# Sliding-window attention and token MLP, two layers: block-diagonal head pairs, 64-key blocks, transposed outputs, and one scheduled dependency graph

## The chip, the core and the metric

The kernel runs on one core of a Trainium2 chip. The metric is the device time of one execution in microseconds (us). A core has five engines that run on their own and meet through semaphores: TensorE (PE in the profile, its weight loads PEld), VectorE (DVE), ScalarE (ACT), GpSimd (POOL) and SyncE (SP), which issues most of the DMA here. The profile also gives the clock that TensorE was granted, as a share of full speed.

## The reference, cut to what matters

All data is bfloat16. Tokens S = 2048, model width D = 512.

```python
def _A_ref(x, wqkv, wo):                    # attention
    H = 32; Dh = D // H; W = 256            # 32 heads of 16; a query sees itself and the 255 tokens before it
    q, k, v = split_heads(x @ wqkv)
    scores = einsum("bhqd,bhkd->bhqk", q, k) * Dh ** -0.5
    p = softmax(where(mask, scores, -1e9))
    return merge_heads(einsum("bhqk,bhkd->bhqd", p, v)) @ wo

def _B_ref(x, w1, b1, w2, b2):              # MLP over the token axis
    h = layernorm(x)
    u = gelu(einsum("bsd,sf->bdf", h, w1) + b1)      # S -> F = 1792
    return transpose(einsum("bdf,fs->bds", u, w2) + b2)

x = A_x
x = x + _A_ref(layernorm(x), ...); x = x + _B_ref(layernorm(x), ...)
x = x + _A_ref(layernorm(x), ...); x = x + _B_ref(layernorm(x), ...)
```

The attention works token by token within a window, so its stages can be interleaved over chunks of tokens. The first product of the MLP sums over all tokens: it ends only after the last token of the attention is done.

## The kernel before

A layer is recorded stage by stage: normalisation, transposes, value, query and key projections for all tokens; then attention; then the output projection; then the MLP. Every engine gets its instructions in the order in which they are recorded, and waits for the semaphores of what it reads.

The attention works on blocks of 128 keys, two heads at a time. Each block meets three query blocks (384 queries), of which the first and the third are masked by triangles. A head has only 16 dimensions, so query and key weights are padded to 32 rows per head, which doubles the projection, and two heads' scores run in two 32-row groups of the array.

```python
                    for uidx, (g, c, hp) in enumerate(units):     # group of 4 heads, key block, pair
                        nj = min(3, NT - c)
                        def f_sc(e, g=g, c=c, nj=nj, hp=hp, st=st):
                            last = None
                            for hl in range(2):
                                hh = 2 * hp + hl
                                last = e.matmul(
                                    SC[:, 2 * st + hl, 0:nj * P],
                                    lhsT=kT_sb[32 * hh:32 * hh + DH, g, c * P:(c + 1) * P],
                                    rhs=qT_sb[32 * hh:32 * hh + DH, g, c * P:(c + nj) * P],
                                    start=True, stop=True, tile_position=(32 * hh, 0))
                        ...   # exp of both heads' scores, 768 columns, on ScalarE
                        ...   # first query block: triangle multiply on VectorE
                        ...   # third query block: affine_select on GpSimd
                        pvq.append((g, c, hp, nj, rs))
                        if len(pvq) > 4:
                            emit_pv(*pvq.pop(0))                  # values, 17 columns per head: 16 and the sum
```

(Cuts are marked with "...".) In the value product the probabilities are the weights that are loaded, and 17 columns per head stream: the output comes with queries on the partitions, and has to be transposed again before the output projection. The gelu of the MLP is made of two ScalarE and four VectorE instructions.

The softmax here doesn't subtract the row's maximum and nothing guards it: scores larger than these inputs give would overflow.

## Time and profile before

The time before is 834.89 us, median of 3 runs (833.97 to 837.9).

| stage of layer 1 | us | what fills it | granted clock |
|---|---|---|---|
| normalisation, transposes, projections | 0 to 112 | loads, then TensorE | 1.00 |
| attention | 112 to 290 (178) | ScalarE | 0.50 |
| output projection | 290 to 314 (24) | VectorE (21.1 us busy) | 0.91 |
| normalisation | 314 to 325 (11) | VectorE | 0.70 |
| MLP | 325 to 432 (107) | TensorE | 0.98 |

The page of the kernel before, part 2. The span is cut into 40 slices, and each digit is the busy share of an engine in tenths; the row PEclk is the granted clock in tenths.

```profile
PE   0499989999999985989968998999999999499898
...
DVE  6740036666666695444557000666666667834322
ACT  0026699999999842330010667999999994233100
...
PEclk9999975555555598999987999555555557899999
```

TensorE looks busy from end to end. But the clock row has two stretches of 5, and in just those ScalarE is at 9: these are the two attentions. The same is told by busy time per stretch. Columns are busy us with the number of instructions for PE, PEld, DVE, ACT and POOL, then granted clock, DMA share, GB/s.

```profile
core 0: us, PE busy (x) PEld busy (x) DVE busy (x) ACT busy (x) POOL busy (x), PEclk, DMA share, GB/s
20.00:110.00 90.00, 76.89 (x368) 36.35 (x368) 27.69 (x63) 38.98 (x67) 0.00 (x0) 1.00 0.00 1
112.00:290.00 178.00, 174.53 (x1958) 85.01 (x1959) 114.15 (x512) 172.97 (x258) 90.98 (x224) 0.50 0.05 13
290.00:314.00 24.00, 20.79 (x120) 10.00 (x117) 21.14 (x43) 10.31 (x18) 0.00 (x0) 0.91 0.00 1
325.00:432.00 107.00, 97.94 (x443) 43.43 (x441) 48.02 (x104) 21.55 (x33) 0.00 (x0) 0.98 0.44 118
```

In attention ScalarE is busy 173 of 178 us. In all other stages it has time, and in attention TensorE works at half clock on little. The timeline of the attention (start, duration, instructions merged, with the count last) shows the pace.

```profile
179.56 7.14 ACT L409 ACTIVATE pT<-SC 128x768 bf16<-128x768 f32 x10
179.72 0.50 PE L399 MATMUL SC<-qT,kT 16*128 16x384 bf16 x2
...
180.15 0.33 PE L366 MATMUL OA<-v,pT 128*128 128x17 bf16 x6
...
180.42 0.50 PE L399 MATMUL SC<-qT,kT 16*128 16x384 bf16 x2
```

Two 384-column scores overlap in 0.50 us, and the six value matmuls follow 0.43 us after the scores start. Ten exponentials take 7.14 us; less the 0.81 us of the last one, nine periods are 6.33 us, so the period of a unit is 0.70 us, one exponential of 768 columns. The groups of instructions give the cost of one: busy us in all, mean ns of one, then idle time before.

```profile
L409 ACT ACTIVATE pT<-SC 128x768 bf16<-128x768 f32 x448 | 316.8, 808 | 4.4 <-PE SC L399 4.4
...
L334 PE MATMUL prj<-xhT,wq_sb 128*128 128x512 bf16 x256 | 65.7, 379 | 0.0
```

### The profile page before, as it was taken

How to read it: one execution, taken by the hardware profiler on the slowest of the kernel's cores; microseconds unless marked ns; L12 is line 12 of the kernel's file. 1: busy time of each engine (PE TensorE's matmuls, PEld its weight loads, DVE VectorE, ACT ScalarE, POOL GpSimd, SP SyncE). 2: the span in 40 equal slices, each digit the busy share in tenths (PEclk: the TensorE clock that was granted, in tenths of full speed). 3: DMA queues.
4: the chain of work that ended last, by engine and by line, in shares of the span. 5: the costliest groups of instructions: out<-in, count | busy, mean ns of one | idle time of the engine just before them, and what ended most of it. 6: DMA issues, size and time to landing. Idle time of an engine off the chain costs nothing. (4 is left out here: it accounts for less than half of the span.)

```text
span 836.1 us, 16132 instructions
## 1 busy us (share of the span) xinstructions
PE 749.4 (90%) x5824; PEld 354.5 (42%) x5824; DVE 432.2 (52%) x1482; ACT 491.1 (59%) x752; POOL 193.7 (23%) x463
## 2 busy tenths in 40 slices
PE   0499989999999985989968998999999999499898
PEld 0244434444444442434434443444444444244343
DVE  6740036666666695444557000666666667834322
ACT  0026699999999842330010667999999994233100
POOL 5000035555555300000000000555555550000000
PEclk9999975555555598999987999555555557899999
DMA  9000030000000001563500002100000000036446
GB/s 201 0 1 1 1 101 2 2 2 2 2 3 2 2 0 28 154 159 89 157 19 1 1 1 60 42 3 2 2 2 2 2 2 1 1 101 168 109 138 189
DMA packets 67773, 36.69 MB, mean 44 GB/s; under 512 B 4720, under 2 KB 67184, under 8 KB 67696
## 3 DMA queue, kind: packets, MB, share of 16 engines
q1 hardware_dynamic: 63824, 35.65, 15.6%
q0 software_dynamic: 3872, 0.02, 1.1%
q8 instruction: 48, 0.79, 0.4%
q14 instruction: 29, 0.24, 0.1%
HBM read 33.56 MB, written 2.10 MB: 43 GB/s over the span
## 5 line engine op out<-in xcount | busy, mean ns | idle before, releaser
L409 ACT ACTIVATE pT<-SC 128x768 bf16<-128x768 f32 (+2 forms) x512 | 344.7, 768 | 6.1 <-PE SC L399 4.4
L420 POOL TENSOR_SCALAR_AFFINE_SELECT pT<-pT 128x256 bf16<-128x256 bf16 x448 | 182.0, 406 | 497.7 <-DVE pT L415 497.7
L415 DVE TENSOR_TENSOR pT<-pT,mall 128x256 bf16<-128x256 bf16 x512 | 149.2, 294 | 229.6 <-ACT pT L409 217.5
L399 PE MATMUL SC<-qT,kT 16*128 16x384 bf16 (+2 forms) x1024 | 244.1, 474 | 9.5 <-ACT pT L409 5.1
L366 PEld LDWEIGHTS OA<-v,pT 128*128 128x128 bf16 x2880 | 115.7, 105 | 157.8 <-POOL pT L420 133.9
L366 PE MATMUL OA<-v,pT 128*128 128x17 bf16 x2880 | 163.0, 179 | 1.2 <-PE OA L366 0.2
L498 PE MATMUL uacc<-xh_sb,w1buf 128*128 128x512 bf16 x448 | 101.4, 390 | 18.1 <-DVE xh_sb L274 17.8
L539 PE MATMUL yacc<-uT,w2buf 128*128 128x512 bf16 x448 | 99.2, 384 | 8.8 <-DVE uT L518 6.5
L342 ACT ACTIVATE qT<-prj 128x512 bf16<-128x512 f32 x64 | 38.2, 597 | 65.2 <-PE prj L334 65.2
L498 PEld LDWEIGHTS uacc<-xh_sb,w1buf 128*128 128x128 bf16 x448 | 44.6, 100 | 74.9 <-issue 24.3
L539 PEld LDWEIGHTS yacc<-uT,w2buf 128*128 128x128 bf16 x448 | 43.9, 99 | 64.1 <-issue 9.7
L399 PEld LDWEIGHTS SC<-qT,kT 16*128 16x128 bf16 x1024 | 52.7, 99 | 32.2 <-ACT pT L409 6.8
L334 PE MATMUL prj<-xhT,wq_sb 128*128 128x512 bf16 x256 | 65.7, 379 | 0.0
L334 PE MATMUL prj<-xhT,wk_sb 128*128 128x512 bf16 x256 | 65.7, 379 | 0.0
L383 DVE TENSOR_TENSOR o<-OA,rtmp 128x64 bf16<-128x64 f32 x256 | 57.5, 225 | 8.9
L544 DVE SCALAR_TENSOR_TENSOR x_sb<-yacc,b2col,x_sb 128x512 bf16<-128x512 f32 x32 | 24.0, 751 | 65.2 <-PE yacc L539 65.2
L305 PE MATMUL trp<-ident,xh_sb 128*128 128x128 bf16 x128 | 16.5, 310 | 39.5 <-DVE xh_sb L274 27.8
L342 ACT ACTIVATE kT<-prj 128x512 bf16<-128x512 f32 x64 | 38.2, 597 | 17.0 <-PE prj L334 17.0
L256 DVE BATCH_NORM_STATS2 stats<-x_sb 128x6 f32<-128x512 bf16 x64 | 44.0, 688 | 6.5 <-DMA x_sb<-in_A_x_dram 4.9
L503 ACT ACTIVATE t0b<-uacc,b1col 128x512 bf16<-128x512 f32 x28 | 19.2, 687 | 45.7 <-PE uacc L498 45.7
L379 DVE RECIPROCAL rtmp<-OA 128x4 f32<-128x4 f32 x256 | 45.0, 176 | 0.8 <-PE OA L366 0.3
L453 PE MATMUL yp<-wo_sb,oTt 128*128 128x512 bf16 x128 | 37.0, 416 | 6.4 <-DVE x_sb L457 5.8
(42 smaller groups left out, 348.3 us busy)
## 6 DMA issues: line engine op xcount, KB each, us to landing
w1buf<-in_B_w_dram SPq DMA_DIRECT2D x14, 1024.0 KB, 6.1
w2buf<-in_B_w_dram SPq DMA_DIRECT2D x16, 896.0 KB, 5.4
x_sb<-in_A_x_dram SPq DMA_DIRECT2D x4, 512.0 KB, 5.5
out_dram<-x_sb SPq DMA_DIRECT2D x16, 128.0 KB, 2.4
wstage<-in_A_wqkv_dram SPq DMA_DIRECT2D x1, 1024.0 KB, 9.1
wv_sb<-in_A_wqkv_dram SPq DMA_DIRECT2D x1, 512.0 KB, 10.0
wo_sb<-in_A_wo_dram SPq DMA_DIRECT2D x1, 512.0 KB, 10.4
b1col<-in_B_b_dram POOLq DMA_DIRECT2D x1, 7.0 KB, 6.5
```

Of the source, the lines that this page charges most:

```text
L256: S_.op("vector", lambda e, t=t: e.bn_stats(stats[:, t, :], x_sb[:, t, :]), reads=[R(f"x_t{t}")], writes=[R(f"stats{t}")])
L334: last = e.matmul(prj[:, ps, :], lhsT=w_sb[:, c, tq * P:(tq + 1) * P], rhs=xhT_sb[:, c, tb * 512:(tb + 1) * 512], start=(c == 0), stop=(c ...
L342: S_.op("scalar", lambda e, tq=tq, tb=tb, dstT=dstT, ps=ps: e.activation(dstT[:, tq, tb * 512:(tb + 1) * 512], prj[:, ps, :], ACTF.Copy), ...
L366: last = e.matmul(OA[:, slot, hh * (DH + 1):(hh + 1) * (DH + 1)], lhsT=pv[:, hl, j, :], rhs=v_sb[:, c, hidx * (DH + 1):(hidx + 1) * (DH + 1)],
L379: S_.op("vector", lambda e, slot=slot: e.reciprocal(rtmp[:, 0:4], OA[:, slot, 0:4 * (DH + 1)].rearrange("p (h e) -> p h e", e=DH + 1)[:, : ...
L383: S_.op("vector", lambda e, slot=slot, g=g, qb=qb: e.tensor_tensor(o_sb[:, qb, g * 64:(g + 1) * 64].rearrange("p (h e) -> p h e", h=4), OA ...
L399: last = e.matmul(SC[:, 2 * st + hl, 0:nj * P], lhsT=kT_sb[32 * hh:32 * hh + DH, g, c * P:(c + 1) * P], rhs=qT_sb[32 * hh:32 * hh + DH, g, ...
L409: S_.op("scalar", lambda e, nj=nj, rs=rs, st=st: e.activation(pT[:, rs, 0:2 * nj * P].rearrange("p (h n) -> p h n", h=2), SC[:, 2 * st:2 * ...
L415: return e.tensor_tensor(v, v, mall[:, :, 0, :], op=ALU.mult)
L420: return e.affine_select(v, v, pattern=[[0, 2], [-1, P]], compare_op=ALU.is_ge, fill=0.0, base=-1, channel_multiplier=1)
L498: last = e.matmul(uacc[:, us, :], lhsT=w1buf[:, b, sc, tt * P:(tt + 1) * P], rhs=xh_sb[:, sc, :], start=(sc == 0), stop=(sc == NT - 1))
L539: last = e.matmul(yacc[:, ys, :], lhsT=w2buf[:, b, fc, stt * P:(stt + 1) * P], rhs=uT_sb[:, fc, :], start=(fc == 0), stop=(fc == NFT - 1))
```

## The change

The intent is to do less work and to have every engine work in every stage.

1. Heads come in pairs. Keys are kept block-diagonally, 64 keys of one head beside 64 keys of the other, so that 32 rows hold two heads with no padding, and a score matmul gives 2 x 64 keys for N queries. Query and key projections halve.
2. Key blocks have 64 keys, so that fewer masked columns are computed: the exponential streams 307 thousand columns per partition in both layers, not 369 thousand.
3. The values and a block of ones are the loaded weights and the probabilities stream: outputs are transposed already, and the denominators come out spread over the rows. Division is Ln, then Exp(-x), then a multiply. Four 32-column groups of the array work on four head pairs.
4. Attention goes in chunks of 512 tokens. Projections of later chunks, output projections of earlier ones and the MLP outputs of the layer before are recorded as "filler" for TensorE.
5. Smaller changes: gelu is one ScalarE instruction, GpSimd's masks go to VectorE, the results of the query and key projections are copied out by VectorE and no longer by ScalarE, and the inverse root of the normalisation is a power on GpSimd.
6. All operations go into one graph with estimated costs, and a list scheduler sets the order of each engine before the program is built. At each step it takes the operation that can start first, and scores go before values, values before fillers.

The diff, cut to its core:

```diff
-class Sched:
+class Graph:
+    def schedule(self):
+        ...
                if m < INF and (best is None or m < best[0]):
                    pick = None
                    for o, t in zip(cand[e], ests):
                        if t <= m:
                            pr = (o.prio if o.prio is not None else ready[o.idx], o.idx)
                            if pick is None or pr < pick[0]:
                                pick = (pr, o)
+        ...
-                                    lhsT=kT_sb[32 * hh:32 * hh + DH, g, c * P:(c + 1) * P],
-                                    rhs=qT_sb[32 * hh:32 * hh + DH, g, c * P:(c + nj) * P],
+                                for j, q0, n, c0 in runs:
+                                    tkk, jj = tk(j)
+                                    for i, r in enumerate(rr):
+                                        last = e.matmul(
+                                            PS[:, 2 * ts.slot + i, c0 * 64:(c0 + n) * 64],
+                                            lhsT=kbd[32 * r:32 * r + 32, tkk.slot, o, jj, :, :].rearrange("p h n -> p (h n)"),
+                                            rhs=qT[32 * r:32 * r + 32, tq.slot, o, q0 * 64:(q0 + n) * 64],
+                                            start=True, stop=True, tile_position=(32 * r, 0), skip_group_check=True)
+        ...
-                                        OA[:, slot, hh * (DH + 1):(hh + 1) * (DH + 1)],
-                                        lhsT=pv[:, hl, j, :],
-                                        rhs=v_sb[:, c, hidx * (DH + 1):(hidx + 1) * (DH + 1)],
+                                for dst, den in ((tO, False), (tDen, True)):
+                                    for r in range(4):
+                                        tp, ln = lane[(k, r)]
+                                        w = onesbd[:] if den else vbd[:, tkk.slot, jj, 4 * o + r, :]
+                                        last = e.matmul(
+                                            PS[32 * r:32 * r + 32, 4 + dst.slot, q0 * 64:(q0 + n) * 64], lhsT=w,
+                                            rhs=pt[:, tp.slot, ln, c0 * 64:(c0 + n) * 64],
+                                            start=st, stop=True, tile_position=(0, 32 * r), skip_group_check=True)
+        ...
+            prepare(0)
+            prepare(1)
+            for m in range(NC):
+                tos[m] = attention(m, tqs[m], tks)
+                wo_block(m, tos[m]) if m == NC - 1 else None
+                if m + 2 < NC:
+                    prepare(m + 2)
+                if m < NC - 1:
+                    wo_block(m, tos[m])
-        layer_A(0)
-        layer_B(0)
-        layer_A(1)
-        layer_B(1)
```

The value projection is part of it: it puts the two heads of a pair on the two halves of the partitions, with 64-column tiles.

```python
                for hf in range(2):
                    def f_v(e, hf=hf):
                        last = None
                        for c in range(4):
                            for sc in range(2):
                                tok = (2 * sp + sc) * 64
                                last = e.matmul(
                                    PS[64 * hf:64 * hf + 64, 4 + ft.slot, sc * 256:(sc + 1) * 256],
                                    lhsT=xhT[:, tx.slot, c, tok:tok + 64],
                                    rhs=wqkv[:, c, 1024:1536].rearrange("p (r h e) -> p r h e", h=2, e=16)[:, :, hf, :],
                                    start=(c == 0 and sc == 0), stop=(c == 3), tile_position=(0, 64 * hf),
                                    skip_group_check=True)
                        return last
                    op("tensor", f_v, ...)      # cut
```

## The prediction

> **What bounds it now.** The stages run one after another. By busy time per stretch and the timeline, each layer pays about 85 us of normalisation, transposes and projections (first scores at 110 us), 178 us of attention, 24 us of output projection, 10 us of normalisation gap and 107 us of token MLP. In attention ScalarE is full (10.0 of every 10 us): exponentials of 768 columns (808 ns busy) start every 703 ns. TensorE shows as busy too, but at a granted clock of 0.50 and with little in it: two row-packed 384-column scores overlap in 0.50 us. In projections and MLP TensorE is the bound, at clock 1.00, 216 ns per 512-column matmul (four in 0.86 us).
>
> **What the change removes.** Query/key projections without padding: 512 matmuls become 256 (-55 us of TensorE at full clock), and 128 evictions of 597 ns leave ScalarE for VectorE. 64-key blocks: the exponential streams 307 thousand columns, not 369 thousand; 288 calls of 1024, at 703 + 256 x 0.833 = 916 ns (estimate), and some smaller, 137 us a layer, with 32 Ln/Exp calls about 155 us. GpSimd masks and 128 output transposes go. Gelu becomes one ScalarE call.
>
> **What it adds.** Value projection with 64-wide tiles: 512 x 256 columns, twice the stream (+27 us). GpSimd block-diagonal copies, 128 of about 630 ns (from affine selects, 292 ns at 128 and 406 at 256 elements). TensorE in attention at full clock, per layer: scores, two row groups abreast, 32 us; values plus a ones matmul, four column groups abreast, 32 us if packing is perfect. The Trainium skill (TensorE: Matmul & The Clock Gate, Measured speedup vs the span model) gives 3.07x for four row tiles and 2.38x for three column tiles, and no run here shows column packing, so I take 90 us for both with small-matmul overheads. Fillers: 72 us. So some 160 us, and 48 more for MLP output in layer 2. VectorE gets about 150 us a layer. All three engines are loaded nearly alike; I expect the greedy static order to lose 10 to 20%.
>
> **Sum.** Start 17; attention with everything inside 185; last output projection and normalisation, partly hidden, 8; MLP first half 51; layer 2's MLP outputs, preparation and attention merged, 235; 8; 51; 53; end 4: 612 us. The gain is overlap.
>
> **Clock.** The skill's clock-gate part says a busy array is ungated; the trace agrees for dense stretches (1.00) and shows 0.50 in sparse attention. With fillers and full-column values I expect 0.85 or more in the new attention. At 0.50, attention would take 320 us and the gain would vanish.
>
> Predicted 612 us, 8 in 10 within 555 to 690. Faster by over 2%: 0.95; within 2%: 0.02; slower: 0.03.
>
> **What would show it.** First scores before 22 us. Exponentials of 1024 start-to-start near 0.92 us when fed; ScalarE about 370 us busy in total, VectorE 320, GpSimd 110. ScalarE 80 to 90% busy in the first attention, lower in the second, which is TensorE-bound. Mean granted clock over 0.9. Attention of layer 1 takes 170 to 205 us, of layer 2 210 to 260. TensorE dominates the end of the chain of waits, with short DMA waits on MLP weights.
>
> **What would make it wrong.** The clock at half in attention; column-packed matmuls that don't run abreast (over 60 us more per layer); drains at each switch between tilings; VectorE late in freeing PSUM, so that fillers stall; GpSimd copies slower than 630 ns and slowing VectorE.

## More of the kernel before

Sessions differ a little: the kernel before gave medians of 834.6 to 837.9 us from one session to the next, so differences of under 3 us between runs of different sessions are not read.

## The result, and the profile after

The changed kernel takes 610.0 us (median of 4, 605.25 to 611.55), the kernel before 836.39 us in the same rounds. The ratio is 0.727 with a 95% interval of 0.723 to 0.731. Ratios here are the mean time of one kernel's fast runs over that of the other's in the same rounds, so they are not quite the ratio of the medians. The prediction was 612 us.

The page of the changed kernel, part 2:

```profile
PE   4879999999998989989899999999998799998797
...
DVE  5984565765784220036766555874568423001122
ACT  0677798798989411110795996099767951111000
...
PEclk9987999999995799999999999999999579999899
```

The two stretches of 5 in the clock row are gone but for a slice or two each, and only the MLPs, with ScalarE at 1, can still be told apart by eye. By stretches (columns as before; the last of the first attention's exponentials of scores ends at 202.2 us, those of the second run from 292.4 to 493.7 us):

```profile
17.80:203.00 185.20, 170.56 (x2572) 86.21 (x2592) 119.15 (x246) 157.89 (x182) 69.13 (x109) 0.92 0.09 23
203.00:265.50 62.50, 59.89 (x289) 25.49 (x292) 7.30 (x17) 11.68 (x17) 3.02 (x8) 0.98 0.38 101
292.00:475.00 183.00, 173.23 (x2424) 81.87 (x2456) 120.69 (x237) 140.58 (x164) 57.57 (x98) 1.00 0.10 27
475.00:493.00 18.00, 14.55 (x200) 6.23 (x204) 6.17 (x12) 15.90 (x19) 1.05 (x2) 0.51 0.01 2
```

The first attention takes 185 us, hardly more than the 178 us of before, but holds nearly all of its layer's projections and most of the output projection. In the second (292 to 475 us) TensorE is busy 173 of 183 us and ScalarE 141: TensorE has become the bound, with MLP outputs of layer 1 as more filler. The last 18 us of each attention are different: clock 0.51, and VectorE is busy only 6.2 of 18 us (shown for the second). The chain of waits that ended last says the same in shares of the span:

```profile
PE 66%; ACT 15%; DVE 11%; DMA 2%; POOL 2%; issue 2%; DVEq 0%; POOLq 0%
```

Before, that chain could only be followed back through the last MLP; now it reaches through the kernel, and is TensorE for two thirds. The groups of instructions (busy us, mean ns, idle before) show the new exponential and two GpSimd groups:

```profile
L599 ACT ACTIVATE pt<-PS 128x1024 bf16<-128x1024 f32 x288 | 278.5, 1039 | 100.9 <-PE PS L586 88.1 <-PE PS L647 11.9
...
L510 POOL TENSOR_SCALAR kbd<-stg,par 128x512 bf16<-128x512 bf16 x64 | 49.5, 783 | 76.7 <-DVE stg L507 74.7 <-DVE agg L440 1.6
...
L449 POOL TENSOR_TENSOR rstd<-rstd,mhalf 128x1 f32<-128x1 f32 x64 | 37.3, 586 | 4.1
```

The timeline of TensorE in the second attention shows how the small matmuls run. Each row is a group of matmuls with its start:

```profile
353.93 0.32 PE L647 MATMUL PS<-pt,vbd 128*32 128x320 bf16 x4
354.07 0.31 PE L647 MATMUL PS<-pt,onesbd 128*32 128x320 bf16 x4
354.21 0.26 PE L647 MATMUL PS<-pt,vbd 128*32 128x192 bf16 x4
354.29 0.26 PE L647 MATMUL PS<-pt,onesbd 128*32 128x192 bf16 x4
354.48 0.39 PE L586 MATMUL PS<-qT,kbd 32*128 32x128 bf16 x6
354.80 0.29 PE L647 MATMUL PS<-pt,vbd 128*32 128x256 bf16 x4
```

Four value matmuls of 320 columns start at 353.93 us, and the next four 0.14 us later. A 512-column matmul takes 0.216 us at this clock, so one of 320 columns takes 0.135 us: the four column groups run fully abreast. The Trainium skill (TensorE: Matmul & The Clock Gate, Measured speedup vs the span model) has 2.38x for three column tiles; in this stream it is four for one. But from the start of the last group (354.29 us; 192 columns, 0.08 us) to the scores it takes 0.19 us, 0.11 more than its stream. That is the time of a change of tiling; between full-array matmuls that follow each other, the same difference is 3 ns (median). My own count over the trace, from 292 to 475 us, takes each run of matmuls in one tiling, and subtracts from its length the time of its columns:

```
from          to            changes   median extra ns
32-row        full array       78        111
full array    32-row           79        111
32-row        32-column        53        110
32-column     32-row           50        126
```

The program changes tiling 653 times; at 0.11 us that is an estimated 72 us of TensorE's time in the kernel's 610. The Trainium skill says of it (TensorEngine Tiling (Array Packing), Key Properties): "Changing tiling mode (not just tile) drains the TensorE". The trace agrees and adds the size.

### The profile page after: what moved, and what is told of

Read it like the earlier page. It is cut to its first block, busy times and chain, and to the rows that moved or that the text cites. A ratio compares the mean times of both kernels' runs of the same rounds, so it can differ in the third digit from the quotient of the medians.

```text
span 609.5 us, 13842 instructions
## 1 busy us (share of the span) xinstructions
PE 556.2 (91%) x6171; PEld 262.6 (43%) x6240; DVE 300.4 (49%) x610; ACT 341.9 (56%) x400; POOL 150.0 (25%) x266
## 4 chain that ended last, share of the span: by engine, by line
PE 66%; ACT 15%; DVE 11%; DMA 2%; POOL 2%; issue 2%; DVEq 0%; POOLq 0%
PE PS L721 15%; PE PS L707 14%; ACT pt L599 13%; PE PS L586 10%; PE PS L523 8%; PE PS L647 8%; PE PS L499 7%; DVE stats L438 4%; PE PS L673 2%; DVE x_sb L676 2%; DVE pt L620 1%; POOL rstd L449 1%; DVE pt L618 1%; DMA w1b<-in_B_w_dram 1%; DVE xh_sb L451 1%
## 5 line engine op out<-in xcount | busy, mean ns | idle before, releaser
L599 ACT ACTIVATE pt<-PS 128x1024 bf16<-128x1024 f32 (+1 forms) x304 | 290.7, 1028 | 102.9 <-PE PS L586 90.1
L586 PE MATMUL PS<-qT,kbd 32*128 32x320 bf16 (+4 forms) x1440 | 123.3, 267 | 13.6 <-ACT pt L599 10.5
L721 PE MATMUL PS<-uT,w2b 128*128 128x512 bf16 x428 | 106.4, 384 | 10.7 <-DMA w2b<-in_B_w_dram 5.0
L707 PE MATMUL PS<-xh_sb,w1b 128*128 128x512 bf16 x436 | 101.2, 384 | 3.0 <-DVE xh_sb L451 1.0
L620 DVE TENSOR_TENSOR pt<-pt,ldm 128x1024 bf16<-128x1024 bf16 (+2 forms) x104 | 64.4, 619 | 56.7 <-ACT pt L599 56.5
L647 PE MATMUL PS<-pt,vbd 128*32 128x320 bf16 (+4 forms) x1440 | 87.6, 273 | 4.9 <-DVE pt L618 1.8
L647 PE MATMUL PS<-pt,onesbd 128*32 128x320 bf16 (+4 forms) x1440 | 84.0, 270 | 0.0
L499 PE MATMUL PS<-xhT,wqkv 128*128 128x512 bf16 x229 | 68.3, 391 | 5.6 <-issue 4.0
L510 POOL TENSOR_SCALAR kbd<-stg,par 128x512 bf16<-128x512 bf16 x64 | 49.5, 783 | 76.7 <-DVE stg L507 74.7
L523 PE MATMUL PS<-wqkv,xhT 128*64 128x256 bf16 x512 | 56.8, 281 | 1.5 <-DVE xhT L490 1.0
```

Of the source, the lines that this page charges most:

```text
L499: mm_group(ft, 4, lambda e, c: e.matmul(PS[:, 4 + ft.slot, :], lhsT=wqkv[:, c, which * 512 + o * P:which * 512 + (o + 1) * P], rhs=xhT[:, ...
L510: op("gpsimd", lambda e, h=h: e.tensor_scalar(kbd[:, tk.slot, o, :, h, :], stg[:, ts.slot, :].rearrange("p (s n) -> p s n", n=64), par[:, ...
L523: last = e.matmul(PS[64 * hf:64 * hf + 64, 4 + ft.slot, sc * 256:(sc + 1) * 256], lhsT=xhT[:, tx.slot, c, tok:tok + 64], rhs=wqkv[:, c, 10 ...
L586: last = e.matmul(PS[:, 2 * ts.slot + i, c0 * 64:(c0 + n) * 64], lhsT=kbd[32 * r:32 * r + 32, tkk.slot, o, jj, :, :].rearrange("p h n -> p ...
L599: return e.activation(pt[:, tp.slot, la:lb + 1:lb - la, 0:n], PS[:, 2 * ts.slot:2 * ts.slot + 2, 0:n], ACTF.Exp, scale=SMSCALE)
L620: return e.tensor_tensor(v, v, msk.unsqueeze(1).unsqueeze(1).to_broadcast([P, lanes, n, w]), op=ALU.mult)
```

## The experiments

All gave the reference's result within its tolerance. Times are medians of 4 runs; the ratio is to the kernel before in the same rounds, and the changed kernel has 0.727.

| run | us | ratio | what it does |
|---|---|---|---|
| serial | 758.5 | 0.906 | no interleaving of stages on TensorE |
| act_more | 633.9 | 0.756 | 61 us more of ScalarE |
| pe_more | 655.7 | 0.783 | 64 us more of TensorE |
| dve_more | 610.3 | 0.728 | 69 us more of VectorE |
| valt | 590.5 | 0.708 | value projection's halves alternate |
| last_dup | 620.3 | 0.744 | last chunk's scores twice |
| last_full | 616.3 | 0.736 | last chunk: useless full-array matmuls |
| switch / noswitch | 622.6 / 612.1 | 0.746 / 0.734 | 192 more changes of tiling / none more |
| valt_ylate | 586.1 | 0.700 | valt, last MLP outputs start later |
| spread | 565.9 | 0.676 | valt_ylate, fillers spread into the last chunk |
| unpacked | 621.6 | 0.742 | values: column groups not neighbours |

### Is the gain overlap, or cheaper work?

The theory is that the fillers run in the gaps of the attention; the rival, that the attention and the projections merely became cheaper. A phase number keeps TensorE from starting a filler inside an attention chunk, and the other way round. Nothing else changes.

```diff
                     t = max(ready[o.idx], free[e])
+                    if e == "tensor" and o.phase != now:
+                        t = INF
...
+                g.phase += 1
                 tos[m] = attention(m, tqs[m], tks)
+                g.phase += 1
```

> Edit: TensorE may not mix stages: it finishes all projections and fillers recorded before an attention chunk, then that chunk alone, then the fillers after it. The instructions, their number and their costs stay. Theory (the gain is overlap: fillers run in the gaps of an attention that ScalarE paces, and they keep the clock up): about 755 us, 720 to 800, granted clock near 0.5 inside the attention chunks. Rival (the attention and the projections simply got cheaper, and the interleaving matters little): under 680 us.

It took 758.5 us. Of the 226 us that the change gained, 148 come from interleaving, and 78 are left when the new arithmetic runs stage by stage. Busy time per stretch of this run: preparation alone, one attention chunk's middle, and the MLP.

```profile
90.00:100.00 10.00, 9.95 (x67) 5.65 (x69) 7.13 (x12) 0.00 (x0) 8.81 (x14) 1.00 0.01 2
230.00:270.00 40.00, 34.07 (x488) 14.88 (x484) 11.85 (x20) 34.12 (x39) 0.00 (x0) 0.50 0.01 2
280.00:330.00 50.00, 48.45 (x218) 20.95 (x220) 1.53 (x6) 9.40 (x14) 1.55 (x4) 1.00 0.47 126
```

In the chunk ScalarE is busy 34 of 40 us, at clock 0.50 and with TensorE "busy" 34 of 40 us as well. In the preparation ScalarE has nothing to do, and in the MLP 9 of 50 us. So a stage-by-stage order pays for both engines in turn. What the half clock alone costs here no run shows; as ScalarE is busy 85% of the chunk, at most the other 15% could be won from it.

### Which engine bounds it?

The prediction said that VectorE, ScalarE and TensorE are loaded nearly alike. Three runs add work to one engine each.

```diff
+# act_more: beside each exponential
+op("scalar", lambda e, td=td: e.activation(scr[:, td.slot, 0:128], ident[:], ACTF.Copy), ..., after=[prev_sc[0]])
+# dve_more: beside each exponential, a multiply of 256 columns to scratch on "vector"
+# pe_more, in f_sc:
-for j, q0, n, c0 in runs:
+for j, q0, n, c0 in runs * 2:
```

> Edit: beside each of the 304 exponentials one more ScalarE copy of 128 columns to scratch, 60 to 85 us of ScalarE in all. If ScalarE bounds both attentions: all of it comes back, +60 to +85 us. My theory (ScalarE and TensorE both near full in the first attention, TensorE alone in the second): +20 to +45 us.

> Edit: every score matmul is issued twice, the second overwriting the first with the same values: 57 us more of streaming at full clock, two row groups abreast. My theory (TensorE bounds the second attention and shares the first): +40 to +60 us. If ScalarE alone bounds attention: under +15 us. If a denser array keeps the clock up at the ends of both attentions, some 5 us of it come back.

> Edit: beside each exponential one more VectorE multiply of 256 bf16 columns to scratch, about 0.29 us each, 88 us of VectorE in all. The prediction said all three engines are loaded nearly alike: then +40 us or more. The profile shows VectorE 62 to 65% busy in attention: then +5 to +25 us, by late evictions only.

(The 57 us in the expectation of pe_more are too few: all 307 thousand columns, two abreast, are 64 us at full clock.) ScalarE's busy time rose by 61 us and the kernel took 24 us longer, so 39% of it showed. Of the 64 us of TensorE 46 showed, 71%. Of VectorE's 69 us nothing showed, which is less than I expected. Busy time of dve_more in the two attentions, columns as before:

```profile
17.80:203.00 185.20, 167.90 (x2587) 84.78 (x2608) 154.66 (x398) 157.14 (x182) 75.20 (x109) 0.95 0.09 23
292.00:493.00 201.00, 187.56 (x2640) 87.88 (x2672) 159.17 (x397) 155.82 (x181) 62.83 (x100) 0.97 0.09 25
```

VectorE is at 84% and 79% in these stretches and still costs nothing. TensorE's load comes first, ScalarE's second, and VectorE's does not bound the kernel. "Loaded nearly alike" was wrong. (This is about load alone: nothing waits for the added multiplies. Others do wait for VectorE's own results, which are 11% of the chain above.)

### The value projection

If TensorE is the bound, its cheapest saving counts. In the changed kernel eight matmuls of one 64-column half run before eight of the other, as two operations, and of the 64 operations the scheduler leaves 27 standing alone, with other work before and after. In valt they are one operation, and alternate.

```diff
-                for hf in range(2):
-                    def f_v(e, hf=hf):
-                        for c in range(4):
-                            for sc in range(2):
+                def f_v(e):
+                    for c in range(4):
+                        for sc in range(2):
+                            for hf in range(2):
```

> Edit: the value projection's two 64-column halves alternate matmul by matmul, instead of eight of one half and then eight of the other. Same 512 matmuls, correct result. In the changed kernel's trace they follow each other at 107 to 109 ns for 256 columns, one at a time, 55 us in all. If neighbouring matmuls of different column groups run abreast: about 27 us of TensorE less and, at the 72% of added TensorE time that showed up in pe_more, 12 to 20 us faster. If column groups do not run abreast here: no change.

It took 590.5 us, 19.5 us less (16 by the ratios). TensorE's timeline of the changed kernel in the first preparation, and then that of valt:

```profile
17.72 1.06 PE L523 MATMUL PS<-wqkv,xhT 128*64 128x256 bf16 x8
```

```profile
17.40 1.06 PE L523 MATMUL PS<-wqkv,xhT 128*64 128x256 bf16 x16
```

Eight matmuls of 256 columns take 1.06 us, one after another; sixteen that alternate take 1.06 us too. The prediction had this cost right ("twice the stream, +27 us") and did not see that the added 27 us were only a matter of order.

### The clock at the end of each attention

The theory was that the clock falls there because TensorE has too little to do once the fillers are used up. last_dup gives it more of the same, last_full gives it full-array work.

```diff
 # last_dup, in f_sc
-for j, q0, n, c0 in runs:
+for j, q0, n, c0 in runs * (2 if m == NC - 1 else 1):
 # last_full, in f_sc, before the scores, which overwrite it
+if m == NC - 1:
+    e.matmul(PS[:, 2 * ts.slot, :], lhsT=ident[:], rhs=qT[:, tq.slot, o, :], start=True, stop=True, ...)
```

> Edit: the score matmuls are issued twice in the last chunk of each layer alone, 17 us more of streaming at full clock. If the granted clock falls to 0.5 there because the array has too little to do: the clock stays up and the time is the same or up to 8 us shorter, with more work. If the work just adds: +5 to +15 us.

> Edit on the changed kernel: in the last chunk of each layer one useless 512-column matmul on the full array before each score group, 40 a layer, 9 us of streaming at full clock. The counterpart of last_dup, where twice the row-packed scores left the clock at 0.5. If full-array work is what holds the clock: over 0.8 in the last chunk, and less than the 10 us that last_dup cost, perhaps nothing. If the clock stays at 0.5: +15 us or more.

Busy time per stretch, columns as before, at the ends of both attentions: first the changed kernel, then last_dup, then last_full.

```profile
190.00:200.00 10.00, 8.44 (x124) 3.69 (x120) 3.06 (x5) 8.49 (x11) 0.00 (x0) 0.50 0.01 2
480.00:490.00 10.00, 9.13 (x140) 4.13 (x136) 3.40 (x6) 8.49 (x11) 0.00 (x0) 0.50 0.01 2
```

```profile
195.00:205.00 10.00, 9.43 (x140) 5.21 (x138) 2.63 (x4) 7.60 (x10) 0.00 (x0) 0.50 0.01 2
490.00:500.00 10.00, 9.70 (x148) 5.24 (x140) 2.64 (x4) 7.60 (x9) 0.00 (x0) 0.50 0.01 2
```

```profile
200.00:210.00 10.00, 9.31 (x115) 3.90 (x115) 2.54 (x5) 7.11 (x9) 0.00 (x0) 1.00 0.01 2
490.00:500.00 10.00, 8.54 (x134) 3.54 (x134) 3.20 (x5) 9.56 (x12) 0.00 (x0) 1.00 0.01 2
```

In last_dup TensorE is busy 9.4 and 9.7 of 10 us and the clock is 0.50 all the same; the work just added 10 us (14 by the ratios). So my theory, put in busy time, fell. In last_full, with fewer instructions, the clock is 1.00, and 17 us more of full-clock streaming cost 6 us. One would conclude that work on the full array holds the clock. But the kept traces show that this is not the rule. In the run switch, told of next, a full-array matmul of 64 columns stands before each score group, and from 490 to 500 us the clock is 0.50. And the changed kernel has stretches of packed matmuls alone at clock 1.00.

What goes with the clock is the share of the array that has been in work. A count over the traces takes each matmul as the time of its columns at full clock (0.216 us for 512), times the share of the array's rows and columns that it uses:

```
run, stretch (us)                       share of the array   clock
before, 130 to 280                      0.11                 0.50
changed kernel, 190-200 / 480-490       0.26 / 0.30          0.50
last_dup, 195-205 / 490-500             0.29 / 0.30          0.50
switch, 490-500                         0.30                 0.50
last_full, 490-500                      0.50                 1.00
spread (below), 160-180 / 440-450       0.59 / 0.58          1.00
changed kernel, 123.84-127.25, packed   0.60                 1.00
```

In all 14 traces the clock changes in steps of 3.4 us. Cut into such steps, a share under 0.28 was followed by clock 0.50 in all 268 cases, a share over 0.44 by 1.00 in all 2009; between them both occur (103 and 130). Of steps with tiles of 32 rows or 32 columns alone, all 36 with a share over 0.38 were followed by 1.00, three of them out of clock 0.50. At half clock the share is held down by the clock itself, but the 52 steps at full clock with a share under 0.28 all lost it. In this measure my theory of too little to do stands after all: last_dup left the share at 0.29 and 0.30. No run sets the share by itself, so this is a regularity of these traces and not a tested cause. The Trainium skill (TensorE: Matmul & The Clock Gate, Part 1) says that the monitor counts "how busy the PE has been recently"; these runs show that the profile's busy time is not what is counted. Useless matmuls don't pay by themselves; spread, below, uses the finding.

### What a change of tiling costs

A 64-column matmul before each score group, on the full array (switch) or in the scores' own tiling (noswitch): same count, same columns.

```diff
 # switch
+e.matmul(PS[:, 2 * ts.slot, 0:64], lhsT=ident[:], rhs=ident[:, 0:64], start=True, stop=True, ...)
 # noswitch
+e.matmul(PS[:, 2 * ts.slot, 0:64], lhsT=ident[32 * rr[0]:32 * rr[0] + 32, :],
+         rhs=ident[32 * rr[0]:32 * rr[0] + 32, 0:64], ..., tile_position=(32 * rr[0], 0))
```

> Edit: before each of the 304 score groups one 64-column matmul on the full array, whose output the scores overwrite. 27 ns of streaming each (8 us), and 845 changes of tiling in TensorE's order instead of 653. If a change costs the 0.11 us that the trace shows between the streams: 192 more are 21 us of TensorE, and this run is 12 to 22 us slower than noswitch.

> Edit: the control of switch: the same 304 extra 64-column matmuls, but in the tiling of the scores (one 32-row group), so TensorE's order has 653 changes of tiling as before. At most 8 us of streaming: +2 to +10 us over the changed kernel.

The two were on the same chip in one session: 622.6 against 612.1 us. So 192 changes cost 10.6 us, or 55 ns each on the clock of the whole kernel. In the trace of switch the step from each added matmul to the scores still takes 0.11 us more than its stream, so about half of it does not show in the kernel's time. It was a little less than I had expected (12 to 22 us).

### Two versions that are faster

valt_ylate adds one edge to the graph. In the changed kernel the first four MLP outputs of the last stage start while the MLP's first half is still running. They hold both weight buffers until it ends, and then TensorE waits (the bracket gives the idle time and what ended it):

```profile
561.08 1.90 PE L721 MATMUL PS<-uT,w2b 128*128 128x512 bf16 x8 [0.78 <-ACT uT L714]
568.01 1.03 PE L721 MATMUL PS<-uT,w2b 128*128 128x512 bf16 x2 [5.03 <-DMA w2b<-in_B_w_dram]
```

```diff
+                after=[last_u[0]] if last and t >= 2 else [])
```

> Edit: valt, and in the last stage the MLP outputs from the third token block on may not start before the last MLP-input matmul. In the changed kernel four of them start early, hold both weight buffers until the stage turns, and then TensorE waits 5 us for the next weights. If that wait is what it costs: 4 to 6 us faster than valt (585 us). If the early outputs filled holes that now open: no gain.

It took 586.1 us, 4.4 us less than valt (6 by the ratios), and the wait is down to 0.68 us:

```profile
534.59 7.16 PE L724 MATMUL PS<-uT,w2b 128*128 128x512 bf16 x32
542.43 2.76 PE L724 MATMUL PS<-uT,w2b 128*128 128x512 bf16 x12 [0.68 <-DMA w2b<-in_B_w_dram]
```

spread acts on the finding that last_full gave about the clock: the output projections of the first three chunks (12 token blocks) are recorded last, and block t may start only after score group 3t of the last chunk.

```diff
-oT = sb("oT", [P, 2, 4, 512])
+oT = sb("oT", [P, 4, 4, 512])
+                    after=[scs[NC - 1][3 * t]] if m < NC - 1 else [])
```

> Edit: valt_ylate, and the output projections of the first three chunks (12 token blocks of four full-array matmuls, 10 us a layer, with their normalisation) are held back and spread over the last chunk's attention, where there was nothing left to fill with and the granted clock fell to 0.5. Four attention-output buffers instead of two. If full-array work keeps the clock up and the early, TensorE-bound part gets shorter: 10 to 20 us faster than valt_ylate, clock near 1.0 in the last chunk. If the clock falls all the same: 0 to 5 us faster, or slower, because more work runs at half clock.

It took 565.9 us, 20 us less than valt_ylate and 44 us less than the changed kernel. Busy time of spread: the end of the first attention, then the second as a whole, then its end.

```profile
160.00:180.00 20.00, 18.90 (x309) 7.50 (x308) 17.65 (x40) 19.93 (x25) 6.02 (x14) 1.00 0.01 2
266.00:455.00 189.00, 185.98 (x2707) 83.02 (x2705) 127.16 (x249) 155.31 (x182) 60.16 (x100) 1.00 0.11 31
440.00:450.00 10.00, 9.40 (x157) 3.85 (x156) 8.88 (x23) 9.88 (x12) 3.37 (x8) 1.00 0.01 2
```

At both ends the clock is 1.00, and ScalarE is busy 20 of 20 and 9.9 of 10 us. TensorE is busy 186 of 189 us in the second attention. Two effects are mixed in this run, the clock at the end and the shorter TensorE-bound part before; it does not part them.

### Column groups that are not neighbours

The prediction said of column packing that no run showed it. unpacked puts the loop over the four column groups outside.

```diff
-for j, q0, n, c0 in runs:
-    for dst, den in ((tO, False), (tDen, True)):
-        for r in range(4):
+for r in range(4):
+    for j, q0, n, c0 in runs:
+        for dst, den in ((tO, False), (tDen, True)):
```

> Edit on the changed kernel: in the value and denominator matmuls the loop over the four 32-column groups goes outside the loops over key blocks and destinations, so that neighbours in TensorE's order share a column group. Same 2880 matmuls, correct result. In the changed kernel's trace four of 320 columns start within 0.14 us, the time of one: 64 us of streaming for both layers. If neighbours of one group go one at a time: up to 256 us of streaming, +130 to +190 us. If the order within a group of matmuls does not matter (they are short, and weight loads bound them): under +30 us.

It cost only 11.6 us. TensorE's timeline:

```profile
355.64 0.20 PE L647 MATMUL PS<-pt,vbd 128*32 128x64 bf16 x1
355.68 0.19 PE L647 MATMUL PS<-pt,onesbd 128*32 128x64 bf16 x1
355.71 0.30 PE L647 MATMUL PS<-pt,vbd 128*32 128x320 bf16 x2
355.75 0.19 PE L647 MATMUL PS<-pt,onesbd 128*32 128x64 bf16 x1
```

In the program, all six matmuls of the first column group come first (64, 64, 320, 320, 128 and 128 columns), then those of the second. In the single records, the first group's start at 355.639, 355.678, 355.707, 355.844, 355.979 and 356.035 us, and the second group's first ones at 355.713, 355.752 and 355.781 us. So matmuls of another column group start ahead of earlier ones that wait for their own, and the four groups run side by side, 74 ns apart. Three waiting matmuls were passed at that point. The Trainium skill (TensorE: Matmul & The Clock Gate, Part 3) calls matmuls "strict FIFO, no reordering"; in this trace starts are not in program order. In the changed kernel four operations of the value projection that stand together, from 274.48 us on, show the same: the second half starts at 274.95 us, when three of the first half's eight are still to start. So, it seems, the six matmuls of a group in unpacked are few enough to be passed in part, while eight of one half in a row leave most of the second half waiting, and alternating them paid. How far ahead a matmul may start no run measures.

## Why the prediction was right

The number was 612 us, the time 610.0. Point by point:

- **Start.** Predicted 17 us, first exponential at 17.8 us. Right.
- **First attention.** Predicted 185 us with everything inside; 17.8 to 203 us is 185 us. Then 8 + 51 us for the rest of the layer's first MLP half; 203 to 265.5 us is 62.5.
- **Second attention.** Predicted 235 us from the end of the first MLP half; 265.5 to 493 us is 227.5. It is TensorE-bound, as said (95% busy from 292 to 475 us, ScalarE 77%). Counted from its first exponential it took 201 us, a little under the range of 210 to 260 us that I gave for it.
- **End.** Predicted 8 + 51 + 53 + 4 = 116 us; 493 to 609.5 us is 116.5.
- **Exponentials.** Predicted 916 ns from start to start; of the 287 intervals between full ones the 158 that waited for little (under 930 ns) are 903 to 920 ns.
- **The gain is overlap.** serial shows it: 148 of the 226 us. The expectation of 755 us for it, by the same sums, met 758.5.
- **The clock.** Predicted over 0.9, measured 0.954. But the reason was not quite right: "fillers and full-column values" were to hold it. At the ends, without fillers, the values did not (clock 0.50, share of the array 0.26 and 0.30); in last_full and spread the share there was 0.50 and more and the clock 1.00.

Some terms were wrong and did not show in the sum.

- "All three engines are loaded nearly alike" fell: 69 us more of VectorE cost nothing.
- "The greedy static order loses 10 to 20%" named a size without a cause. Much of what was lost is TensorE's: changes of tiling (0.11 us each), a value projection that ran one half at a time (16 to 20 us), the half clock at the ends and badly placed fillers (20 us in spread), and early MLP outputs that hold their weights (4 to 6 us). I had listed the changes of tiling among what would make the prediction wrong, and had put 26 us per layer above perfect packing for "small-matmul overheads". By its columns packing is perfect, and the changes (an estimated 36 us a layer from 0.11 us each) take the place of those overheads.
- GpSimd was put at 110 us and took 150: a block-diagonal copy took 752 to 783 ns on average, not 630, and the power of one column for the normalisation 586 ns. GpSimd is 2% of the chain, so little of this showed.
- ScalarE was put at 370 us and took 342, since the overlap of instructions that follow each other was counted in the period and, it seems, forgotten in the busy time: the lengths of its instructions add up to 377 us.

So the forecast was right because the two large facts were: what ScalarE needs per attention, and that the rest of a layer fits beside it at full clock. That it came within 2 us is luck in part: by its own terms, 160 us of TensorE with 10 to 20% lost, the first attention could have been put anywhere from 176 to 192 us (estimate), the loss had no cause behind it, and spread shows that 44 us of the measured time could still be saved.

## What to carry to other kernels

When one stage is bound by one engine and the next by another, first cost each engine over both stages together: the gain from interleaving them (148 us here) can be larger than that from cheaper arithmetic. Once they are interleaved, look again at the engine that became the bound, and add work to each engine in turn to find it, since busy shares of 80% can cost nothing. Keep some fillers, full-array matmuls best, for the end of a stretch of packed ones, so that enough of the array stays in work; put tiles that can run abreast next to each other in one operation, and count the changes of tiling.

## What the Trainium skill lacked or had wrong

- TensorEngine Tiling (Array Packing), Key Properties, says that changing the tiling mode drains TensorE, without a size: 110 to 126 ns over the streams' time here, and 55 ns of kernel time per added change.
- TensorE: Matmul & The Clock Gate, Part 3, says that matmuls start and end in program order. In unpacked, matmuls of a second column group started at 355.713 us ahead of three earlier ones of the first group, which started at 355.844 us and later.
- The same page, Part 1, says that a busy array is ungated, but not what counts as busy. In last_dup the granted clock was 0.50 at 9.4 to 9.7 us busy of 10. The share of the array in work separates the cases: under 0.28 of it the clock that followed was always 0.50, over 0.44 always 1.00.
- The same page, Measured speedup vs the span model, has 2.38x for three column tiles: in a long stream four column tiles of 320 columns took 0.14 us, the time of one.
- GPSIMD Engine Reference has no cost for a power of a single column: 586 ns on average here, against 231 ns for a multiply and add of the same size.
